# A fused state-space convolution and gated MLP: the second half's 32-row exchange by VectorE copies, spare reload buffers, one pool of PSUM banks, some copies moved between engines, and a new order

## The chip, the cores and the metric

One core of one Trainium2 chip. The metric is the device time in microseconds of one execution; runs are given with their median. The engines are named as the profile names them: PE is TensorE, DVE VectorE, ACT ScalarE, POOL GpSimd, SP the sync engine, which here only issues DMA transfers.

## What is computed

The reference, cut to what matters (x is 2048 tokens by 512 channels, N is 128 modes, F is 1792):

```python
xn = layernorm(x)                                    # per token
dt = exp(log_dt)[:, None]
A, Bc, Cc = A_re + 1j*A_im, B_re + 1j*B_im, C_re + 1j*C_im
K = einsum("dn,dnl,dn->dl", Cc, exp((dt*A)[:, :, None] * l), dt*Bc).real   # l = 0..2047
y = causal_convolution(xn, K) + xn * Dskip           # per channel, by FFT of length 4096
h = sigmoid(xn @ w_gate) * (xn @ w_up)
return x + y + h @ w_down
```

## The kernel before

**Two computations share the core.** The gated MLP is four groups of 512 tokens. A group has 14 gate products (line 1012) and 14 up products (line 1027), each of four 128x512 matmuls into one PSUM bank; ScalarE turns a gate bank into a sigmoid in SBUF (line 1021), and VectorE multiplies it with the up bank (line 1042). For the units that the list `UEV` names, ScalarE first copies the up bank into the tile `us_sb` (line 1038), and VectorE reads that copy instead of PSUM. Four down products of 14 matmuls each (line 1065) end a group; outside the last group ScalarE copies them out (line 1098) and POOL issues an accumulating load that adds x (line 1104).

**The convolution** is done by two short transforms with multiplications between them. First the layernorm is applied in place to the tile `xn` (part of one big SBUF tile). Sixteen first transforms (line 677) leave their results in PSUM pairs (two banks); ScalarE copies a pair out (line 683) and SP stores it to `z_scr` in DRAM. Meanwhile a ladder of twelve squarings (lines 652 to 660, casts to bf16 at line 646) and many complex multiplications on VectorE (lines 717 to 723, seeds copied at line 758) build tables of powers in four blocks of channels (`c` 0 to 3). For each block TensorE contracts the tables (line 806), ScalarE copies the result out (line 812), TensorE rearranges it (line 828), ScalarE copies it into `kT` (line 835) and VectorE adds one row (line 841).

Then come sixteen units: eight of the first 256 channels (`p` 0; blocks 0 and 1) and eight of the second half (`p` 1; blocks 2 and 3). One unit:

1. SP loads a piece of `z_scr` into a buffer zx, TensorE transforms it (line 881), ScalarE copies the pair into half of a buffer xx (line 886).
2. The exchange: four DMA transfers of 64 KB on SP copy each block of 32 partitions of that half to the neighbouring block of 32 partitions in the other half.
3. SP loads a constant E; TensorE multiplies it with `kT` (line 899), ScalarE copies the pair to kb (line 901).
4. VectorE multiplies xx by kb (lines 905 and 909), TensorE transforms back (line 922), ScalarE copies the pair to vs (line 926), and SP stores it to `v_scr`.

At the end both halves of v are reloaded (16 transfers of 256 KB), last transforms (lines 980 and 982) add them to the down products, VectorE adds x (lines 995 and 1085), and SP stores the output.

**What sets the order.** Every step is one operation of a plan (`pl.add`): engine, function, dependencies, slots that it takes and gives back. The cost, the priority and the DMA figures that it is given are not used when the kernel is built. The order is written out by hand as the list `ORDER` of 970 operation numbers; each engine gets its operations in that order and works them off one after the other. The plan hands out slots in that order too, first freed first taken: pairs of PSUM (`s`, two), single banks for gate and up products (`gu`, three), one bank for down products and the warming matmuls (`po`), two zx, three xx, two kb. An operation waits where its slot is still in use. Line 404 issues nearly all transfers, so that tiles tell the transfers apart; the eight transfers in flight on SP's queue each have a semaphore of their own, and a ninth waits for the first.

```python
sws = [dma("SP", lambda xx=xx, b=b: xx()[32 * b:32 * b + 32, 1, :, :],
           lambda xx=xx, b=b: xx()[32 * (b ^ 1):32 * (b ^ 1) + 32, 0, :, :], deps=[ex], prio=QP, pkt=2048, hv=0.5)(64 * KB)
       for b in range(4)]
pa_ = pl.add("DVE", 1.14, fpa, [ek] + sws, PKD, acq=[psl])
```

Of the kernel before, what the change touches and what calls it, by code (L numbers as in the profile page):

```python
# [11 lines left out]
F32 = mybir.dt.float32  # L12
# [20 lines left out]
NH = 41  # L33
# [5 lines left out]
NS, NGU, NPO = 2, 3, 1  # L39
# [136 lines left out]
def _consts():  # L176
# [22 lines left out]
UEV = (17, 21, 24, 25, 28, 29, 30, 31, 32, 33, 34, 35, 36, 37, 38, 39, 40, 41, 42, 44, 45, 46, 47, 49, 51)  # L199
ON_ACT = (0, 2)  # L200
ORDER = [
    2, 42, 21, 18, 44, 43, 0, 3, 1, 23, 22, 47, 45, 9, 10, 17, 5, 32, 24, 14, 33, 25, 46, 48, 26, 4, 6, 34, 27, 35, 29,
    28, 36, 37, 38, 39, 19, 30, 31, 40, 41, 619, 620, 631, 632, 621, 90, 87, 88, 49, 89, 50, 53, 662, 633, 663, 55, 92,
    51, 672, 54, 673, 91, 12, 56, 667, 642, 58, 7, 11, 101, 102, 93, 103, 682, 683, 8, 643, 57, 652, 653, 668, 625,
    657, 626, 669, 670, 59, 658, 622, 623, 627, 15, 61, 671, 60, 63, 97, 664, 113, 624, 677, 678, 659, 639, 640, 62,
    660, 665, 94, 95, 666, 100, 661, 64, 52, 637, 104, 638, 105, 687, 688, 679, 96, 66, 680, 98, 641, 681, 647, 628,
    629, 648, 65, 114, 630, 106, 141, 634, 684, 674, 144, 67, 635, 685, 142, 686, 636, 649, 68, 650, 675, 676, 115,
    644, 689, 131, 651, 654, 70, 167, 143, 145, 214, 109, 69, 108, 655, 132, 645, 690, 646, 215, 691, 134, 71, 72, 107,
    168, 656, 169, 216, 73, 99, 768, 725, 692, 217, 170, 171, 146, 135, 773, 769, 74, 76, 75, 693, 116, 770, 694, 110,
    111, 133, 172, 77, 79, 218, 219, 78, 149, 726, 774, 150, 80, 173, 760, 695, 775, 776, 81, 771, 16, 761, 117, 82,  # L210
    83, 147, 700, 174, 118, 119, 772, 701, 85, 718, 151, 728, 702, 175, 123, 84, 177, 185, 148, 122, 152, 186, 777,
    220, 189, 190, 154, 708, 719, 178, 187, 188, 112, 155, 153, 729, 709, 191, 758, 748, 193, 738, 161, 180, 179, 749,
    720, 182, 721, 739, 183, 759, 710, 194, 195, 733, 722, 750, 164, 165, 162, 751, 136, 196, 711, 734, 740, 197, 121,
    139, 712, 752, 763, 198, 201, 181, 741, 742, 764, 163, 753, 754, 176, 140, 723, 735, 755, 756, 137, 736, 724, 199,
    762, 202, 200, 192, 138, 126, 730, 203, 120, 731, 129, 737, 127, 130, 13, 727, 204, 757, 732, 128, 713, 715, 205,
    714, 86, 184, 743, 156, 716, 717, 159, 124, 206, 221, 222, 744, 157, 745, 765, 766, 746, 747, 767, 160, 207, 209,
    208, 224, 794, 824, 232, 261, 226, 703, 262, 233, 236, 230, 234, 235, 231, 237, 225, 210, 240, 227, 263, 264, 241,
    242, 243, 265, 778, 779, 796, 797, 229, 125, 158, 389, 359, 238, 244, 780, 781, 245, 854, 248, 239, 246, 249, 247,
    360, 390, 391, 361, 786, 434, 782, 223, 855, 787, 211, 250, 435, 228, 436, 440, 212, 266, 251, 252, 253, 788, 795,
    267, 213, 254, 256, 255, 268, 798, 814, 257, 258, 825, 271, 364, 365, 308, 269, 279, 309, 280, 362, 366, 259, 815,  # L220
    393, 260, 394, 274, 275, 281, 826, 804, 441, 358, 363, 396, 395, 439, 827, 273, 367, 442, 829, 859, 438, 310, 283,
    282, 284, 311, 285, 437, 368, 287, 272, 426, 830, 860, 805, 369, 312, 370, 288, 828, 289, 449, 443, 789, 444, 290,
    834, 811, 836, 837, 397, 835, 799, 392, 398, 809, 800, 812, 450, 451, 810, 371, 445, 399, 277, 839, 291, 840, 276,
    292, 813, 838, 831, 819, 372, 832, 295, 820, 293, 801, 802, 419, 381, 833, 294, 286, 400, 427, 821, 822, 428, 880,
    844, 278, 297, 313, 454, 296, 298, 314, 823, 420, 421, 166, 704, 401, 881, 402, 453, 841, 456, 457, 856, 455, 374,
    373, 299, 458, 790, 696, 270, 375, 857, 376, 803, 300, 446, 842, 447, 816, 301, 303, 845, 858, 302, 817, 452, 318,
    315, 459, 818, 326, 317, 323, 460, 424, 422, 425, 411, 378, 379, 380, 327, 843, 330, 304, 319, 885, 806, 807, 846,
    328, 329, 331, 847, 471, 423, 808, 429, 920, 382, 851, 320, 403, 334, 886, 849, 383, 404, 335, 430, 461, 321, 336,
    405, 852, 325, 850, 848, 406, 462, 892, 861, 893, 472, 448, 486, 377, 473, 887, 337, 853, 479, 546, 410, 316, 384,
    431, 338, 432, 862, 480, 20, 339, 385, 340, 863, 341, 305, 481, 342, 888, 322, 344, 324, 306, 882, 412, 332, 433,  # L230
# [17 lines left out]
class _Slot:  # L248
    __slots__ = ("pool", "idx")

    def __init__(self, pool):
        self.pool = pool
        self.idx = None

class _Plan:
# [6 lines left out]
    def add(self, eng, cost, fn, deps=(), prio=0.0, acq=(), rel=(), dma=None, mode="F", tab=None, alt=None):  # L262
# [5 lines left out]
        op.seq = len(self.ops)  # L268
        for d in deps:
            if d is not None:  # L270
                d.users.append(op)
                op.left += 1
        self.ops.append(op)
        return op

    def run(self):

        for n in ORDER or range(len(self.ops)):
            op = self.ops[n]
            for s in op.acq:  # L280
# [875 lines left out]
```

## Time and profile before

| | us |
|---|---|
| median of 3 runs (lowest, highest) | 237.1 (236.8, 238.4) |
| the profiled execution | 238.7 |
| its span | 236.9 |
| ACT busy | 183.8 |
| POOL busy | 22.4 |
| 64 exchange transfers of 64 KB, median from issue to landing | 3.0 |
| 16 z reloads of 256 KB, median | 4.3 |
| 16 v stores of 256 KB, median | 3.6 |
| 12 v reloads on SP's queue, median | 5.5 |

An engine's busy time is the union of its instructions' durations; the mean of one instruction, which the groups give in ns, is longer than its share of the busy time where an instruction starts before the one ahead of it has ended. An idle stretch is put down to the event that came last before it. In the chain of waits each line is one step, with its start, its length, and the engine or transfer that it ran on.

### The profile page before, as it was taken

To read this page: it belongs to the slowest core of one execution; us is meant where nothing else is said; L and a number is where in the kernel's file an instruction comes from. 1 tells how busy PE (TensorE), PEld (TensorE's weight loads), DVE (VectorE), ACT (ScalarE), POOL (GpSimd) and SP (SyncE) were. 2 spreads that over 40 slices of the span, in tenths; PEclk is the share of its full clock that TensorE was granted. 3 is DMA by queue.
4 is the path that set the end of the run, shared out by engine and by line. 5 is a ranking of instruction groups with operands and counts; after the bars stand their busy time and mean duration, and the time that the engine had idled before them with its cause. 6 is when DMAs were issued, how large, how long until landed. Compare 5 with 4: busy or idle time off the path is not lost.

```text
span 236.9 us, 5425 instructions
## 1 busy us (share of the span) xinstructions
PE 217.8 (92%) x2093; PEld 111.0 (47%) x2120; DVE 186.3 (79%) x397; ACT 183.8 (78%) x299; POOL 22.4 (9%) x42
## 2 busy tenths in 40 slices
PE   7977999799999999996999999999899979999693
PEld 2443434244444364454655565556544536444252
DVE  2999999999999999997999999994530561681374
ACT  5999999999999996756999999977557859870000
POOL 1212030040000000670030000000010001000000
PEclk9999999999999999999999999999999999999999
DMA  6999614433624375429887348455698499796965
GB/s 186 330 381 371 201 51 141 121 110 111 133 89 136 129 209 153 82 52 296 209 167 198 79 125 237 117 165 136 174 236 233 119 288 239 206 239 189 297 226 177
DMA packets 47739, 43.46 MB, mean 183 GB/s; under 512 B 9569, under 2 KB 40674, under 8 KB 47714
## 3 DMA queue, kind: packets, MB, share of 16 engines
q1 hardware_dynamic: 45618, 40.43, 57.6%
q0 software_dynamic: 864, 1.57, 4.4%
q10 hardware_dynamic: 1232, 1.11, 1.6%
q8 instruction: 16, 0.26, 0.5%
q14 instruction: 9, 0.07, 0.1%
HBM read 25.28 MB, written 12.06 MB: 158 GB/s over the span
## 4 chain that ended last, share of the span: by engine, by line
PE 46%; ACT 18%; DMA 15%; DVE 14%; issue 4%; SPq 2%; DVEq 0%; ACTq 0%
PE bank L1027 11%; PE bank L1012 11%; PE bank L1065 8%; PE pair L899 7%; DMA big<-z_scr 5%; DVE hT_sb L1042 4%; ACT hT_sb L1021 4%; PE pair L922 3%; PE pair L806 3%; DMA big<-in_A_u_dram 2%; DMA big<-v_scr 2%; SPq L404 2%; ACT big L683 2%; DMA v_scr<-big 2%; PE pair L881 2%
## 5 line engine op out<-in xcount | busy, mean ns | idle before, releaser
L1012 PE MATMUL bank<-xnT,wg_sb 128*128 128x512 bf16 (+1 forms) x223 | 53.6, 368 | 5.9 <-DMA xnT<-x_scr 1.8
L1027 PE MATMUL bank<-xnT,wu_sb 128*128 128x512 bf16 x214 | 53.4, 379 | 1.1 <-ACT hT_sb L1021 0.4
L1065 PE MATMUL bank<-wd_sb,hT_sb 128*128 128x512 bf16 (+1 forms) x234 | 50.9, 367 | 0.2
L1012 PEld LDWEIGHTS <-wg_sb 128*128 128x128 bf16 x236 | 22.0, 97 | 29.9 <-issue 5.7
L1065 PEld LDWEIGHTS <-hT_sb 128*128 128x128 bf16 x238 | 22.6, 98 | 25.7 <-issue 2.4
L1021 ACT ACTIVATE hT_sb<-bank 128x512 bf16<-128x512 f32 x56 | 32.9, 608 | 1.5 <-PE bank L1012 1.5
L905 DVE TENSOR_TENSOR big<-big 128x2048 bf16<-128x2048 bf16 x16 | 19.6, 1224 | 16.9 <-PE pair L922 10.1
L1027 PEld LDWEIGHTS <-wu_sb 128*128 128x128 bf16 x224 | 20.8, 98 | 25.5 <-issue 3.7
L717 DVE TENSOR_TENSOR big<-big 128x1024 bf16<-128x1024 bf16 (+4 forms) x40 | 25.9, 648 | 0.9 <-ACT big L758 0.5
L1042 DVE TENSOR_TENSOR hT_sb<-hT_sb,bank 128x512 bf16<-128x512 bf16 x31 | 20.6, 680 | 6.9 <-PE bank L1027 6.7
L718 DVE TENSOR_TENSOR big<-big 128x1024 bf16<-128x1024 bf16 (+4 forms) x40 | 25.9, 647 | 0.0
L886 ACT ACTIVATE big<-pair 128x1024 bf16<-128x1024 f32 x16 | 16.3, 1024 | 5.4 <-PE pair L881 5.4
L899 PE MATMUL pair<-big 128*128 128x256 bf16 x160 | 19.7, 273 | 0.0
L901 ACT ACTIVATE big<-pair 128x1024 bf16<-128x1024 f32 x16 | 16.3, 1022 | 2.9 <-PE pair L899 2.6
L899 PEld LDWEIGHTS <-big 128*128 128x128 bf16 x160 | 15.5, 98 | 4.7 <-issue 0.2
L926 ACT ACTIVATE big<-pair 128x1024 bf16<-128x1024 f32 x16 | 16.3, 1029 | 1.1 <-PE pair L881 0.5
L722 DVE TENSOR_TENSOR big<-big 128x512 bf16<-128x512 bf16 (+4 forms) x40 | 16.9, 423 | 0.2
L723 DVE TENSOR_TENSOR big<-big 128x512 bf16<-128x512 bf16 (+4 forms) x40 | 16.9, 422 | 0.0
L1038 ACT ACTIVATE us_sb<-bank 128x512 bf16<-128x512 f32 x25 | 14.9, 600 | 2.5 <-PE bank L1027 2.3
L683 ACT ACTIVATE big<-pair 128x1024 bf16<-128x1024 f32 x16 | 16.1, 1047 | 0.4 <-DMA z_scr<-big 0.4
L774 ACT ACTIVATE sq_sb<-big 128x256 bf16<-128x256 bf16 (+2 forms) x20 | 12.9, 646 | 3.9 <-DVE big L723 2.9
L646 ACT ACTIVATE big<-big 128x512 bf16<-128x512 f32 x24 | 13.8, 640 | 0.0
(106 smaller groups left out, 270.4 us busy)
## 6 DMA issues: line engine op xcount, KB each, us to landing
big<-c_E SPq DMA_DIRECT2D x16, 320.0 KB, 3.5
z_scr<-big SPq DMA_DIRECT2D x16, 256.0 KB, 2.6
big<-z_scr SPq DMA_DIRECT2D x16, 256.0 KB, 4.3
big<-big SPq DMA_DIRECT2D x64, 64.0 KB, 3.0
v_scr<-big SPq DMA_DIRECT2D x16, 256.0 KB, 3.6
big<-v_scr SPq DMA_DIRECT2D x12, 256.0 KB, 5.5
big<-in_A_u_dram SPq DMA_DIRECT2D x4, 512.0 KB, 8.0
wu_sb<-in_B_w_up_dram SPq DMA_DIRECT2D x2, 896.0 KB, 10.6
```

The costliest lines, as they stand in the source:

```text
L683: ev = pl.add("ACT", 0.90, lambda sl=sl, zs=zs: S.activation(out=zs().rearrange("p j d -> p (j d)"), in_=two(sl), func=ACT.Identity), [fx_ ...
L717: V.tensor_tensor(out=wide(outp), in0=wide(lo), in1=mre, op=ALU.mult)
L718: V.tensor_tensor(out=wide(tb()), in0=wide(lo), in1=mim, op=ALU.mult)
L722: V.tensor_tensor(out=outp[:, :, :, 0, :], in0=outp[:, :, :, 0, :], in1=tb()[:, :, :, 1, :], op=opr)
L723: V.tensor_tensor(out=outp[:, :, :, 1, :], in0=outp[:, :, :, 1, :], in1=tb()[:, :, :, 0, :], op=opi)
L899: T.matmul(two(sk)[:, o:o + DW], es()[:, g, kt, :], kT[p][:, kt, :], start=kt in (0, NKT - 1), stop=kt >= NKT - 2)
L905: V.tensor_tensor(out=pp().rearrange("p q h m -> p (q h) m"), in0=xx().rearrange("p q h m -> p (q h) m"), in1=kb()[:, 0:2 * DW].unsqueeze( ...
L1012: T.matmul(bank(sl)[:, c0:c1], w[:, kt, k * 128:(k + 1) * 128], xnT[:, grp, kt, c0:c1], start=(kt == 0), stop=(kt == KT - 1))
L1021: S.activation(out=hT_sb[:, hs.idx, k % 2, :], in_=bank(sl), func=ACT.Sigmoid)
L1027: T.matmul(bank(sl), wu_sb[:, kt, k * 128:(k + 1) * 128], xnT[:, grp, kt, :], start=(kt == 0), stop=(kt == KT - 1))
L1042: V.tensor_tensor(out=h(), in0=h(), in1=us_sb[:, us.idx, :] if on else bank(sl), op=ALU.mult)
L1065: T.matmul(bank(po)[:, 0:c[1] - c[0]], hT_sb[:, hts[k // 2].idx, k % 2, jj * 128:(jj + 1) * 128], wd_sb[:, k, c[0]:c[1]], start=first and ...
```

## The change

- The exchange of the second half's units (`p` 1) is four VectorE copies instead of four transfers; the first half's stays on SP.
- When the last table contraction has run, memory that the tables used is handed to the pools: a fourth buffer xx and eight more zx. A unit takes its xx when it copies into it, no longer when z is loaded. The reloaded v are laid out by half first, so that the extra zx lie where the second half's v go.
- The bank `po` joins the pool `gu` (four banks) for gate, up and down products and the warming matmuls.
- Copies that ScalarE made go through `pl.copy`, which puts an operation on VectorE if its number is in `ON_DVE`: four casts of the ladder, seven of twelve layernorm applications, nine small table copies and three pair evictions of the second half (two into xx, one into vs). `UEV` has 37 units instead of 25.
- The last down products no longer name the last transform back as a dependency.
- `ORDER` is new (946 operations). Of what moves: SP loads x first and the first parameters fourth; the load of w_down stands behind the first x and z stores and the first transposing load; the third set of five warming matmuls stands before the first gate; three down products of the third group stand before the last table contraction instead of behind it.

```diff
-NS, NGU, NPO = 2, 3, 1
+NS, NGU = 2, 4
-UEV = (17, 21, 24, 25, 28, 29, 30, 31, 32, 33, 34, 35, 36, 37, 38, 39, 40, 41, 42, 44, 45, 46, 47, 49, 51)
+UEV = (0, 2, 4, 5, 9, 10, 14, 15, 16, 18, 19, 20, 23, 24, 25, 27, 28, 29, 30, 31, 32, 33, 34, 36, 37, 38, 39, 40, 41, 42, 43, 44, 47, 50, 51, 52, 54)
+ON_DVE = (54, 57, 60, 84, 96, 107, 108, 110, 120, 121, 123, 167, 177, 179, 180, 182, 214, 230, 273, 308, 481, 565, 573)
...
+    def copy(self, nc, cost, out, in_, *args, **kw):
+
+        get = lambda v: v() if callable(v) else v
+        dve = len(self.ops) in ON_DVE
+
+        def fcopy():
+            if dve:
+                nc.vector.tensor_copy(out=get(out), in_=get(in_))
+            else:
+                nc.scalar.activation(out=get(out), in_=get(in_), func=ACT.Identity)
+        return self.add("DVE" if dve else "ACT", cost, fcopy, *args, **kw)
...
-            if i >= LN_ACT:
+            dve = i < LN_ACT or len(pl.ops) in ON_DVE
+            if not dve:
...
+            if dve:
+                V.tensor_copy(out=W[p][:, k], in_=cur[:, :, DW * p:DW * p + DW])
...
+    kgen[3][0].rel += tuple(_Slot(k, i) for k, n, m in (("xx", 3, 4), ("zx", 2, 10)) for i in range(n, m))
...
             lx = dma("SP", zx, z_v[:, u, :, dsl], deps=fx_st + xn_free, prio=QP,
-                     acq=[xsl, zsl], pkt=512, hv=0.49)(256 * KB)
+                     acq=[zsl], pkt=512, hv=0.49)(256 * KB)
...
+            ex = pl.copy(nc, 0.91, lambda xx=xx: xx()[:, 0].rearrange("p h (g d) -> p g h d", g=2),
+                         lambda sl=sl: two(sl).rearrange("p (g h d) -> p g h d", g=2, h=2), [mm], QP, acq=[xsl], rel=[sl])
+            half_of = lambda xx, b, q: xx()[32 * b:32 * b + 32, q, :, :]
+            if p == 0:
+                sws = [dma("SP", lambda xx=xx, b=b: half_of(xx, b, 1), lambda xx=xx, b=b: half_of(xx, b ^ 1, 0), deps=[ex], prio=QP,
+                           pkt=2048, hv=0.5)(64 * KB) for b in range(4)]
+            else:
+                def f_sw(xx=xx):
+                    for b in range(4):
+                        V.tensor_copy(out=half_of(xx, b, 1), in_=half_of(xx, b ^ 1, 0))
+                sws = [pl.add("DVE", 1.5, f_sw, [ex], QP)]
...
-    vall = at(0, [8, NP, 2, 2, DW])
-    vps = [[vall[:, t, p] for t in range(8)] for p in range(NP)]
+    vall = at(0, [NP, 8, 2, 2, DW])
+    vps = [[vall[:, p, t] for t in range(8)] for p in range(NP)]
...
-            pos = [_Slot("gu" if late and jj % 2 else "po")] + [_Slot("gu")] * last
+            pos = [_Slot("gu") for _ in range(1 + last)]
...
-                            prods + [l_wd] + ([md] if jj else []) + ([mv_] if late else []) + pre_, DP, acq=[] if last else [po],
+                            prods + [l_wd] + ([md] if jj else []) + pre_, DP, acq=[] if last else [po],
```

## The prediction

> **What bounds the kernel now.** I read the page's totals and slices first, then busy time by stage, then the chain of waits, then the groups by shape.
>
> ```profile
> PE 217.8 (92%) x2093; PEld 111.0 (47%) x2120; DVE 186.3 (79%) x397; ACT 183.8 (78%) x299; POOL 22.4 (9%) x42
> ...
> PE   7977999799999999996999999999899979999693
> ...
> DVE  2999999999999999997999999994530561681374
> ACT  5999999999999996756999999977557859870000
> ```
>
> TensorE is the bound: its 217.8 us of matmul stay whatever the change does, so only its 19.1 us of idle time can be won, 3.6 of it after the last matmul. VectorE is full until about 165 us and then half empty; ScalarE is full until 88.
>
> ```profile
> core 0: us, PE busy (x) PEld busy (x) DVE busy (x) ACT busy (x) POOL busy (x), PEclk, DMA share, GB/s
> 0.00:13.68 13.68, 11.20 (x54) 5.14 (x55) 8.50 (x30) 10.57 (x19) 2.46 (x12) 1.00 0.86 278
> 13.68:44.10 30.42, 26.21 (x138) 12.06 (x140) 29.82 (x63) 30.33 (x51) 4.40 (x6) 1.00 0.66 213
> ...
> 136.34:160.14 23.80, 23.39 (x343) 13.36 (x346) 23.67 (x52) 21.53 (x37) 0.89 (x3) 1.00 0.57 159
> 160.14:211.50 51.36, 48.41 (x581) 26.86 (x588) 23.87 (x39) 36.51 (x49) 1.73 (x2) 1.00 0.78 207
> 211.50:236.90 25.40, 19.73 (x120) 9.56 (x121) 11.37 (x15) 1.93 (x3) 0.00 (x0) 1.00 0.71 224
> ```
>
> Stages, cut at the first gate matmul (13.68), the end of group 0 (44.10), the last table matmuls (160.14) and the last unit's product (211.50). Up to 160.14 TensorE idles 10.5 us, in the second half 3.0, in the tail 5.7. The granted clock is 1.00 in all of them.
>
> ```profile
> 162.10 4.38 DMA big<-z_scr
> ...
> 190.77 1.24 DVE big L905
> ...
> 212.87 4.46 DMA v_scr<-big
> ...
> 217.96 5.22 DMA big<-v_scr
> ```
>
> The chain of waits names what TensorE waited for late: a reload of z (two buffers only; 1.02 us lost at 166.5), a product behind the exchange (1.35 us lost at 192), and at the end the last v store and its reload.
>
> **The start.** SP issues its loads in another order: the first parameter load moves from first to fourth, behind x tiles 0 to 7. It took 3.1 us. With it 1,408 KB are queued; the present fifth load has 1,440 KB queued and took 6.5 us (issued 2.6, landed 9.1). So I put it at 8.7 us instead of 3.9. ScalarE's queue still has exp and sin ahead of the two evictions into xnT: exp 0.63, two VectorE multiplies 1.3, exp 0.61, table load 1.28, four sin steps 2.47: 6.3 us, so the evictions start at 15.0 instead of 12.72. Cost 2.3 us; bounds 0 (3.1 us as now) and 5 (9.9 us, the second parameter load). Five warming matmuls (1.2 us, formerly at 151) fill part of it. The load of w_down moves behind the first x and z stores and the first transposing load. By the durations of ScalarE's queue SP reaches it at 33 us. As it took 15.9 us among the other loads, and its 1,792 KB are 5 us at the 330 to 381 GB/s that the page gives for 6 to 24 us, it lands between 40 and 49; the first down group comes at about 44. I take 41 and no cost, since no other large load is left by then; the late end would cost 5.
>
> **Before the last table.** ScalarE loses 4 casts (2 x 0.575), 7 normalisations (0.825), 9 small table copies (0.43) and 3 pair evictions (1.02), and gains 12 us copies (0.60): -4.6 -5.8 -3.9 -3.1 +7.2 = -10.2 us. The rest of that comes in the first 88 us, where it is full: ahead of the first table's eviction its queue is 4 us shorter.
>
> VectorE, up to the end of the last table, gains the casts (nearest row 128x512 f32 at 0.42, so 4 x 0.84; up to 0.69 if they go as two-operand f32), the normalisations (the same instruction as L543, 0.37 busy), the small copies (nearest two-operand row 0.29; I take 0.24), and 11 products fewer from PSUM (0.665) with 12 more from us (0.416): 3.4 + 2.6 + 2.2 - 7.3 + 5.0 = +5.9 us (between +4 and +8). The last table ended on VectorE at 159.7, so it ends at 165.6, or 164 if the 1.45 us wait of L841 at 111.9 goes. TensorE has three down groups more (3.02 each) and one gate and one up fewer (0.86) queued ahead of it: +7.3. So VectorE's delay is covered if TensorE idles no more than 7 to 8 us there.
>
> TensorE's idle time up to there was 10.5: 2.5 before 13.68, 4.2 to 44.10, 3.8 later. The start makes 3.6 of the 2.5. The 1.76 us wait for xnT goes: its store came at 33.7, 19 us after the evictions into xnT, and now has some 9 us of ScalarE work behind them ahead of it; one z store fewer stands before its transposing load on SP. Of 2.4 us of waits for a free bank I take half, since gate and up products now rotate over four banks, and down groups share them, so a bank held 3.0 us by a down group can also cost as much. Of the 1.47 us before the second selection, two thirds. Sum 10.5 + 1.1 - 1.8 - 1.2 - 1.0 = 7.6. TensorE reaches the last table at 149.7 (its busy time so far) + 7.3 + 7.6 = 164.6, VectorE at 164 to 165.6: I take 164.8.
>
> **Second half.** It loses the three down groups and gains an up: 48.4 - 9.1 + 0.9 = 40.2 us of TensorE. Eight z loads may run ahead (five slots are used past the first two, all freed by the last table matmuls), so the z wait goes; 32 SP issues of 0.5 us and their 3.0 us landings go. In their place VectorE makes 32 copies of 32x1024.
>
> ```profile
> L905 DVE TENSOR_TENSOR big<-big 128x2048 bf16<-128x2048 bf16 x16 | 19.6, 1224 | 16.9 <-PE pair L922 10.1 <-ACT big L901 3.0 <-DMA big<-big 2.9
> ...
> L718 DVE TENSOR_TENSOR big<-big 128x1024 bf16<-128x1024 bf16 x16 | 11.0, 688 | 0.0
> ...
> L543 DVE TENSOR_SCALAR big<-big,ln_m_f,ln_ri_f 128x512 bf16<-128x512 bf16 x4 | 1.5, 409 | 0.0
> ...
> L604 DVE TENSOR_SCALAR big<-big 128x512 f32<-128x512 f32 x1 | 0.4, 419 | 0.0
> ```
>
> No row is a wide bf16 copy. Two operands of this length take 0.69, one operand of half of it 0.41 (0.33 start to start). So four copies cost 1.3 to 2.75 us; one element a cycle, as L995 from PSUM with 1.22 for 1024, would make 4.9. I take 2.0, between the two SBUF rows, since a copy has no second stream and no scalar to read. Until the last unit VectorE then has 10 x 1.225 + 10 x 0.68 for products, 8 x 2.0, three evictions at 1.2, six products 3.0 and a small row 0.3: 42 us, where it had 23.9 in a longer stage. TensorE's 40.2 and about 2.5 of waits make 42.7. Among these: the first pair eviction on VectorE waits for unit 8, whose z load SP issues only behind a v store, about when the table matmuls start (4.4 us of load, 2.7 of cover). Behind it in VectorE's queue stands the row addition that all K products of this half wait for: up to 2 us. They are level; each 0.1 us more per exchange past 2.1 adds 0.8 us. Last unit at 207.5 (was 211.5).
>
> [...]
>
> **Tail.** Behind the last product TensorE has one gate and two ups where it had two ups, so 0.9 us more of the v store and reload is hidden (0.93 was idle at 220.7), and 0.9 us more work is left: nothing either way. The 25.4 us stay. The new layout of the v buffers lets z lie where the second half's v come last; it adds no instruction. On POOL the prefix sums (some 6 us) move behind the last memset at about 165 and are needed some 25 us later: nothing.
>
> Span 207.5 + 25.4 = 232.9. The profiled execution took 238.7 (span 236.9 and 1.8 around it), so it would be 234.7, 4.0 less. The median of the runs is 237.1, 1.6 below the profiled one: 237.1 - 4.0 = 233.1.
>
> **Rivals.** *VectorE becomes the bound* of the second half: slower. It speaks for it that it has 42 us against 42.7, in a fixed order, where a late exchange also holds the products, and two evictions that free a PSUM pair. It decides from 2.1 us per exchange; at 2.75 the time is 238.3, from 2.9 it is over 1% slower, at 3.3 it is 242.7, at 4.9 some 255. Against it: VectorE's half idle stage, and rows that all lie below 0.7. *The new order does not fit the chip*: the late parameters cost 2.3 us (up to 5) and the shared banks win nothing, so TensorE idles as before up to the last table; VectorE's +5.9 then sets it at 165.6 to 167.5, and the time is 235 to 240, 237 likeliest. For it: ScalarE and VectorE have no slack in the first 88 us. *The exchange was hidden anyway*: then only the earlier work counts; z's 1.0 and the product's 1.35 stay lost, 235.4.
>
> **How the numbers follow.** 1% (2.4 us) is what can be told from no change. The forecast, 229 to 234.7, gets 0.55. The order that does not fit 0.22: 0.05 faster, 0.12 within, 0.05 slower. VectorE as the bound 0.16: 0.03 within, 0.13 slower. The hidden exchange 0.07: 0.03 faster, 0.04 within. Sums: faster 0.63, same 0.19, slower 0.18. About 0.07 lies below 229 and 0.12 above 240, so the range is 229 to 240.
>
> **What would show it.** First gate matmul near 16.0 us, not 13.7; no wait for xnT near 44; the last table's matmuls at 164 to 166 with some 7.6 us of TensorE idle before; copies of 32x1024 at 0.45 to 0.55 us; VectorE over 90% full from there to the last unit's product at 207 to 208; about 25 us behind it. I am wrong if the copies take over 0.55 us or the last table comes after 168.

## The result and the profile after

The changed kernel takes 236.06 us (median of 20 runs, 234.39 to 238.51) beside 237.36 us for the kernel before (also 20 runs): ratio 0.994, 95% interval 0.991 to 0.997. The prediction was 233.1. The forecast gain of 4 us became 1.3, a third of it.

The profiled execution took 238.2 us with a span of 236.4. The page of the changed kernel, its totals and slices:

```profile
PE 220.5 (93%) x2092; PEld 112.3 (47%) x2120; DVE 205.9 (87%) x456; ACT 175.4 (74%) x284; POOL 19.4 (8%) x42
...
PE   7959999999899999999999999999699999997794
...
DVE  3799999999979999999999998998679989960474
...
PEclk9999999999999999999999999999889999999799
```

VectorE is now full into the second half, as meant. New are two dents in the row of the granted clock, near 170 and 222 us; the kernel before had none. Busy time by stage, cut as before (first gate matmul, end of group 0, last table matmuls, end of the last unit's product):

```profile
core 0: us, PE busy (x) PEld busy (x) DVE busy (x) ACT busy (x) POOL busy (x), PEclk, DMA share, GB/s
0.00:16.41 16.41, 12.60 (x58) 5.59 (x60) 10.86 (x35) 10.68 (x19) 2.46 (x12) 1.00 0.89 300
...
163.22:207.85 44.63, 41.59 (x544) 23.64 (x549) 39.06 (x70) 32.29 (x43) 4.17 (x9) 0.96 0.76 206
207.85:236.40 28.55, 22.22 (x127) 10.88 (x125) 12.71 (x17) 2.59 (x4) 0.00 (x0) 0.94 0.52 166
```

| stage, us | predicted | changed kernel | kernel `both` (below) |
|---|---|---|---|
| to the first gate matmul | 16.0 | 16.41 | 15.35 |
| to the last table matmuls | 148.8 | 146.81 | 147.67 |
| second half | 42.7 | 44.63 | 42.02 |
| behind the last product | 25.4 | 28.55 | 24.16 |
| span | 232.9 | 236.40 | 229.20 |

Up to the last table the kernel is 1.6 us ahead of the prediction. It loses 1.9 in the second half and 3.15 in the tail. TensorE's waits, largest first (total, how often, longest), name both places:

```profile
PE pair L991 <- DMA big<-v_scr: 2.9, 1, 2.9
...
PE pair L838 <- issue: 1.3, 1, 1.3
```

In the timeline the first loss lies inside the last selection (the matmuls that rearrange a table result, line 828 before and 838 now), which stops after 50 of 64 matmuls with everything it reads in place; the second ahead of the first last transform:

```profile
166.75 0.74 PE L838 MATMUL pair<-big,sw 128*32 128x96 bf16 x50 [0.51 <-ACT big L285]
168.80 0.35 PE L838 MATMUL pair<-big,sw 128*32 128x96 bf16 x14 [1.31 <-issue]
...
220.02 0.62 PE L991 MATMUL pair<-big 128*64 128x512 bf16 x4 [2.94 <-DMA big<-v_scr]
```

Busy time by stretch behind each of the two; the third column from the end is the granted clock, 0.50 for some 3 us:

```profile
169.80:173.00 3.20, 2.98 (x9) 1.22 (x9) 2.90 (x6) 0.80 (x2) 0.00 (x0) 0.50 0.50 79
```

```profile
221.00:224.00 3.00, 3.00 (x16) 1.57 (x13) 2.19 (x3) 0.00 (x0) 0.00 (x0) 0.50 0.37 110
```

At the clock of 0.50 six gate matmuls (line 1023, from 170.10 us) took 2.77 us, where eight at 1.00 took 1.89 to 1.90 (180.69 and 193.10): half the pace. TensorE then does in 3.2 us what takes 1.6, so by my estimate each fall costs up to 1.6 us. Not every execution has both falls: the two runs whose mean clock was 1.00 had spans of 232.4 and 232.8 us, the six at 0.983 to 0.986, the profiled one among them, had 234.0 to 236.4, so the table shows the losses of a long execution.

### The profile page after: what moved, and what is told of

Same layout as the page of the kernel before. It is cut to its first block, busy times and chain, and to the rows that moved or that the text cites. A ratio compares the mean times of both kernels' runs of the same rounds, so it can differ in the third digit from the quotient of the medians.

```text
span 236.4 us, 5411 instructions
## 1 busy us (share of the span) xinstructions
PE 220.5 (93%) x2092; PEld 112.3 (47%) x2120; DVE 205.9 (87%) x456; ACT 175.4 (74%) x284; POOL 19.4 (8%) x42
## 4 chain that ended last, share of the span: by engine, by line
PE 51%; DVE 14%; ACT 14%; DMA 13%; issue 4%; SPq 2%; ACTq 0%; DVEq 0%
PE bank L1076 13%; PE bank L1038 9%; PE bank L1023 9%; PE pair L912 6%; DMA v_scr<-big 5%; PE pair L818 5%; ACT big L285 4%; PE pair L934 4%; ACT big L662 3%; DMA big<-in_A_par_dram 3%; ACT big L668 2%; DVE big L609 2%; DMA big<-v_scr 2%; SPq L416 2%; DMA z_scr<-big 2%
## 5 line engine op out<-in xcount | busy, mean ns | idle before, releaser
L285 ACT ACTIVATE big<-pair 128x1024 bf16<-128x1024 f32 (+2 forms) x73 | 70.7, 986 | 18.4 <-PE pair L818 5.5
L1076 PE MATMUL bank<-wd_sb,hT_sb 128*128 128x512 bf16 (+1 forms) x232 | 50.3, 367 | 0.3
L733 DVE TENSOR_TENSOR big<-big 128x1024 bf16<-128x1024 bf16 (+4 forms) x40 | 25.7, 642 | 0.8 <-ACT big L285 0.5
L1049 ACT ACTIVATE us_sb<-bank 128x512 bf16<-128x512 f32 x37 | 22.6, 614 | 0.8 <-PE bank L1038 0.5
L1053 DVE TENSOR_TENSOR hT_sb<-hT_sb,us_sb 128x512 bf16<-128x512 bf16 x37 | 15.2, 415 | 0.5 <-ACT us_sb L1049 0.5
L903 DVE COPY big<-big 32x1024 bf16<-32x1024 bf16 x32 | 13.4, 419 | 0.6
L1006 DVE TENSOR_TENSOR big<-pair,glu_sb 128x1024 bf16<-128x1024 f32 x4 | 4.8, 1221 | 10.2 <-PE pair L991 10.2
L1053 DVE TENSOR_TENSOR hT_sb<-hT_sb,bank 128x512 bf16<-128x512 bf16 x19 | 12.9, 681 | 0.6 <-PE bank L1038 0.3
L934 PE MATMUL pair<-big 64*64 64x512 bf16 (+1 forms) x256 | 13.1, 327 | 0.1
```

The source lines that it names most:

```text
L285: nc.scalar.activation(out=get(out), in_=get(in_), func=ACT.Identity)
L733: V.tensor_tensor(out=wide(outp), in0=wide(lo), in1=mre, op=ALU.mult)
L934: T.matmul(two(sv)[o:o + 64, DW * (2 * g + y):2 * DW * (g + 1)], mab[b:b + 64, 2 * u + g, q, :], pq()[b:b + 64, q, ch] if y else pp()[b:b ...
L1049: S.activation(out=us_sb[:, us.idx, :], in_=bank(sl), func=ACT.Identity)
L1053: V.tensor_tensor(out=h(), in0=h(), in1=us_sb[:, us.idx, :] if on else bank(sl), op=ALU.mult)
L1076: T.matmul(bank(po)[:, 0:c[1] - c[0]], hT_sb[:, hts[k // 2].idx, k % 2, jj * 128:(jj + 1) * 128], wd_sb[:, k, c[0]:c[1]], start=first and ...
```

## The experiments

**The tail.** The first suspicion fell on the new layout. The last transform of a block of tokens reads both halves of v with one access. In the old layout that is 4 KB in one piece; in the new one it is a range of 16 KB and more, which takes in other blocks. In the program as compiled, the first last transform waits for seven transfers' semaphores in the changed kernel and for three in the old layout. `v_by_token`:

```diff
-zx=[OFF["zs"], OFF["zs"] + 2 * KB] + [16 * KB + 2 * KB * i for i in range(8)])
+zx=[OFF["zs"], OFF["zs"] + 2 * KB] + [2 * KB + 4 * KB * i for i in range(8)])
-    vall = at(0, [NP, 8, 2, 2, DW])
-    vps = [[vall[:, p, t] for t in range(8)] for p in range(NP)]
+    vall = at(0, [8, NP, 2, 2, DW])
+    vps = [[vall[:, t, p] for t in range(8)] for p in range(NP)]
-            T.matmul(o[64 * j:64 * j + 64, :], s2[:, r, :], vall[:, ps, t, j, r, :], ...
+            T.matmul(o[64 * j:64 * j + 64, :], s2[:, r, :], vall[:, t, ps, j, r, :], ...
```

> The changed kernel with one thing undone: the v buffers lie token block by token block again (both halves of a block side by side), and the extra z places take the second half's 2 KB of each block instead of one 16 KB region. No instruction is added or taken away. Theory (a wait by address range): in the changed kernel the last transform of block 2 reads one range that reaches over the places of blocks 3 to 7 of the first half and 0 to 2 of the second, so it waits for the reload of block 1, the last one issued, and lands at 220.02; with the old layout it waits for its own two loads (the second half's block 2 was issued at 213.01 and took 4.8 us), so it starts near 218, idle before it falls from 2.94 to about 1 us, the granted clock behind it stays at 1.00 where it was 0.50 for 3.2 us, and the stretch from the last unit's product to the end is about 25 us instead of 28.55. Time 232.3 to 233.5, 2.5 to 3.7 less than the changed kernel's 236.06, ratio to before near 0.981. Rival A (the reload is late by itself, since eight loads share the DMA engines): the first last transform still starts at 219.5 or later and the time stays at 235.5 to 236.5. Rival B (the clock falls for another reason than this wait): the start moves to 218 but the clock still falls to 0.5 behind it; 234 to 234.8.

Measured: 233.39 us, ratio 0.987 (0.982 to 0.991). The timeline of `v_by_token` in the tail:

```profile
208.92 6.22 PE L1076 MATMUL bank<-wd_sb,hT_sb 128*128 128x512 bf16 x28
215.58 0.62 PE L991 MATMUL pair<-big 128*64 128x512 bf16 x4 [0.45 <-DMA big<-v_scr]
217.03 0.59 PE L991 MATMUL bank<-big 128*64 128x512 bf16 x3 [0.83 <-DMA big<-v_scr]
```

The one wait of 2.94 us has become small ones (a third, of 0.52, follows), each for the block that is needed next, and the clock stays at 1.00. The median is inside the expected span, the ratio a little above it. The wait by address range is the cause; rivals A and B are out. Its size varies, though. The four profiles with the new layout wait 2.94, 2.67 (`par_first`), 2.9 (`warm_tail`, most of it filled) and 1.24 us ahead of the first last transform; the nine with the old layout wait 0.45 us there (`v_by_token`) or not at all. The short one is `fetch_shift`:

```profile
215.83 0.62 PE L991 MATMUL pair<-big 128*64 128x512 bf16 x4 [1.24 <-DMA big<-v_scr]
```

There the clock stays at 1.00 as well, and from the last product to the end it takes 25.7 us, as long as `v_by_token`. The nine with the old layout take 24.0 to 25.7 us, so the new one cost less than 2 us in that execution and 2.9 us or more in the profiled one, the fall of the clock included.

**The clock by itself.** `warm_tail` leaves the layout and the wait, and fills most of the wait with matmuls:

```diff
+    def f_wt():
+        for _ in range(10):
+            T.matmul(bank(wtl), glu_sb[:, 0, 0:128], glu_sb[:, 0, :], start=True, stop=True)
+    pl.add("PE", 1.5, f_wt, (), 0, acq=[wtl], rel=[wtl])
```

> The changed kernel with ten more matmuls of 128x512 on constant weights, whose result nobody reads, put into TensorE's wait ahead of the first last transform (2.1 us of work). The wait for the reload stays. Theory (an idle stretch of nearly 3 us makes the granted clock fall): the first last transform starts near 220.0 as before, but the clock stays at 1.00 behind it, so the end comes 1.4 to 1.7 us sooner: 234.2 to 234.8. Rival A (the clock falls for another reason, the load on the chip or the narrow matmuls): it falls to 0.5 as before and the time is 236 or a little over. Rival B (the end is bound by the output stores, so TensorE's slow stretch costs nothing): clock 1.00 and still 236.

Measured: 235.65 us, ratio 0.994 (0.991 to 0.997). The timeline of `warm_tail` at the filled wait, and its busy time by stretch behind it:

```profile
214.93 2.32 PE L1121 MATMUL bank<-glu_sb 128*128 128x512 bf16 x10
217.96 0.62 PE L991 MATMUL pair<-big 128*64 128x512 bf16 x4 [0.71 <-DMA big<-v_scr]
```

```profile
217.90:221.00 3.10, 2.96 (x23) 1.58 (x23) 2.38 (x4) 0.00 (x0) 0.00 (x0) 1.00 0.03 4
221.00:224.00 3.00, 2.92 (x14) 1.13 (x12) 1.19 (x3) 0.00 (x0) 0.00 (x0) 1.00 0.94 302
```

With 0.71 us of the idle stretch left, the clock stays at 1.00, and none of the twelve runs has a mean clock under 0.991, where six of the twenty of the changed kernel have 0.983 to 0.986. So the idle stretch can make the clock fall. It need not: in `par_first` the clock stays at 1.00 behind 2.67 us at the same place.

```profile
220.85 0.62 PE L991 MATMUL pair<-big 128*64 128x512 bf16 x4 [2.67 <-DMA big<-v_scr]
```

The time hardly moves, which misses the expected 1.4 to 1.7 us. In this execution TensorE, at full clock, waited 0.89 us for a later reload instead, and the clock fell at 167 to 172 us as in the changed kernel. How much of the tail's fall the reload would have cost anyway is not settled.

**The stop in the selection.** The kernel before had such a stop too, 1.47 us inside its second selection:

```profile
108.51 0.65 PE L828 MATMUL pair<-big,sw 128*32 128x96 bf16 x43
110.63 0.42 PE L828 MATMUL pair<-big,sw 128*32 128x96 bf16 x21 [1.47 <-issue]
```

Counted in TensorE's compiled order (matmuls and weight loads), the two come ahead of instructions 1723 and 3259, and both numbers leave 187 when divided by 256. `fetch_shift` moves all numbers by 168 without adding columns:

```diff
-                T.matmul(bank(wsl), glu_sb[:, 0, 0:128], glu_sb[:, 0, :], start=True, stop=True)
+                T.matmul(bank(wsl)[:, 0:w], glu_sb[:, 0, 0:128], glu_sb[:, 0, 0:w], start=True, stop=True)
-    warm = [keep_warm(28, -10)]
+    warm = [keep_warm(112, -10, 128)]
```

> The changed kernel with its 28 first warming matmuls of 128x512 cut into 112 of 128x128: the same columns, 168 more instructions (matmuls and weight loads) ahead of everything else on TensorE. Theory (the 1.31 us stop inside the last selection, and the 1.47 us one inside the second selection of the kernel before, are TensorE's sequencer waiting for its next block of instructions: both stops come at an instruction number that leaves 187 when divided by 256, 1723 and 3259, in a stretch where nearly 400 short instructions follow one another while loads fill the DMA engines): with the numbers moved by 168 the boundary falls into the table matmuls, the block after it is needed only behind the selection, and no stop of over 0.5 us is left in the selections; the granted clock stays at 1.00 from 163 to 175 where the profile showed 0.50 for 3.2 us. The profiled execution's second half (last table to last unit's product) is 42 to 43 us instead of 44.6; the median of the runs moves by 0 to -0.8, since most runs of the changed kernel have only one fall of the clock, the one in the tail. Rival A (the stop belongs to the instruction, an operand or a semaphore): it stays behind the 50th matmul of the last selection. Rival B (it belongs to the load on the DMA engines alone): a stop of 1 us or more comes anywhere in 166 to 169 us.

Measured: 234.47 us, ratio 0.987 (0.983 to 0.991). The second and the last selection in the timeline of `fetch_shift`:

```profile
111.30 0.82 PE L838 MATMUL pair<-big,sw 128*32 128x96 bf16 x59
112.56 0.24 PE L838 MATMUL pair<-big,sw 128*32 128x96 bf16 x5 [0.44 <-issue]
...
166.80 0.87 PE L838 MATMUL pair<-big,sw 128*32 128x96 bf16 x64 [0.30 <-ACT big L285]
```

So the last selection runs through. A short stop has come in the second one, ahead of instruction 1981, which leaves 189. With the instructions that only wait for a semaphore counted too, all three places leave the same remainder, 194: the new place is that of a boundary to the instruction. All three profiles that keep the changed kernel's numbers up to there (`v_by_token`, `warm_tail`, `par_first`) stop behind the same 50th matmul, for 1.88, 1.06 and 2.06 us, so it is in every profile seen, and the gain (0.7% by the ratios, 1.6 us by the medians) is larger than the 0.8 us expected at most. Rival A is out. So is B as it stands, for the stop keeps to an instruction number; that it needs loaded DMA engines as well is left open.

`both` has the two edits together.

> The changed kernel with the old v layout (z places moved into the second half's places of it) and the 28 warming matmuls cut into 112, that is the edits of v_by_token and fetch_shift together. Theory (the false wait for v and the stop at an instruction block are two separate losses that the prediction did not have): no stop over 0.5 us in the last selection, the waits ahead of the first last transforms together below 2 us, the granted clock at 1.00 in all stages; second half 42 to 42.7 us, 25.2 to 26.7 behind it; time 231.5 to 232.8, ratio to before 0.976 to 0.980. Rival (one loss hides the other: when the second half ends sooner, the reload still needs its 10 us behind the last v store, and VectorE, 93% full, takes back the stop): 233.2 to 234, as with either edit alone.

Measured: 230.82 us, ratio 0.973 (0.968 to 0.979): a shorter time than with either edit alone, and shorter than expected. Its second half and tail, busy time by stage:

```profile
163.02:205.04 42.02, 40.59 (x544) 23.52 (x550) 39.52 (x72) 32.24 (x43) 4.82 (x9) 1.00 0.79 221
205.04:229.20 24.16, 20.53 (x125) 9.91 (x125) 12.55 (x17) 2.59 (x4) 0.00 (x0) 1.00 0.59 194
```

The clock is 1.00 throughout, and the two losses do not hide one another: by the ratios the gain over the changed kernel is 2.1%, where each edit alone brings 0.7%. What goes beyond their sum is not clear of the intervals. A stop is left in the second selection, at the place where `fetch_shift` has one:

```profile
112.31 0.24 PE L838 MATMUL pair<-big,sw 128*32 128x96 bf16 x5 [0.90 <-issue]
```

This kernel is faster than the kernel before and the changed one.

**Can the boundary be put where it does no harm?** `best` moves the numbers by 136 (96 warming matmuls of 128x149).

> The kernel of both with the 28 first warming matmuls cut into 96 of 128x149 instead of 112 of 128x128, so that the instruction numbers move by 136 instead of 168. In the profiles so far each stop ends 4.2 to 5.3 us after TensorE passed the instruction number one block (256) earlier; so a stop comes wherever TensorE runs through 256 instructions in less time than that. Theory: by the durations of the matmuls, 168 leaves one such place (118 instructions into the second selection, where both stopped 0.90 us) and 136 leaves none. No stop of over 0.25 us in any selection or table; 0.4 to 1 us less than both's 230.82, ratio to before 0.968 to 0.973. Rival (blocks do not set it; another place takes the stop): one stop of 0.5 us or more elsewhere, and no less time than both.

Measured: 231.11 us, ratio 0.975 (0.970 to 0.980), no better than `both`. In its timeline TensorE stops inside the last table (the profiled execution took 234.1 us, 3.0 more than the median, so the stop need not be as long in all):

```profile
162.11 2.63 PE L818 MATMUL pair<-big 128*32 128x82 bf16 x114 [0.57 <-DVE big L738]
167.03 0.47 PE L818 MATMUL pair<-big 128*32 128x82 bf16 x14 [2.29 <-issue]
```

114 matmuls into the table is instruction 3259 once more, so the place is right and the rule for the length was wrong. The boundary before it was passed at 158.3 us, 8.7 us ahead of the restart and not 4.2 to 5.3. The block itself (one packet of 16 KB on an instruction queue) moved at 164.5 to 165.0 us, while the DMA engines had been idle from 157 to 160: the request went out later than I had it. In this kernel that boundary lies 28 instructions ahead of the table, which waited for VectorE until 162.11; what lets the request go out is not shown.

**Does the stop cost the kernel before anything?** `before_shift` is the kernel before with 122 warming matmuls of 128x117.

> The kernel before the change, with nothing altered but its 28 warming matmuls, cut into 122 of 128x117: the instruction numbers move by 188. Theory (the stop of 1.47 us in its second selection has the same cause): that stop is gone; a shorter one may come in the last table's place, where two boundaries are some 3.5 us apart, if the DMA engines are loaded there. Time 235.9 to 236.8, ratio to before 0.993 to 0.998. Rival (in this kernel the stop is covered, since VectorE's ladder sets the last table): no change, ratio 0.998 to 1.002, with the 1.47 us turned into another wait before the last table.

Measured: 238.42 us, ratio 1.008 (1.005 to 1.011). The second selection runs through, and the next K product (E times `kT`) comes 3 us behind it in the timeline of `before_shift`:

```profile
108.97 0.87 PE L828 MATMUL pair<-big,sw 128*32 128x96 bf16 x64
...
113.08 2.12 PE L899 MATMUL pair<-big 128*128 128x256 bf16 x16 [1.41 <-DMA big<-c_E]
```

The stop was covered there: that product waits for its E load, which did not come sooner. The rival is right in kind. Why this kernel is even slower is open; its first gate came 0.5 us later.

**The start.** `par_first` moves one number, the first parameter load, back to the head of `ORDER`.

> The changed kernel with the first parameter load put back to the head of SP's queue, everything else as it is. Theory (the prediction's: the late parameters cost 2.3 us which nothing takes back, as TensorE is full behind the start): par0 lands near 4 us, the first gate matmul comes at 13.7 to 14.2 instead of 16.4, and the last table matmuls at 161 to 162 instead of 163.2; time 233.7 to 234.5. Rival A (x tiles 0 to 3 come 0.6 us later and their statistics then set the first gate): 15 or later, gain under 1 us. Rival B (ScalarE and VectorE set the pace up to 88 us, so an earlier first gate only moves idle time to later waits for xnT and the table casts): first gate at 14, last table still at 163, time 235.5 to 236.3.

Measured: 237.10 us, ratio 0.996 (0.993 to 1.000). The load landed at 3.94 us and the first gate matmul came at 16.87, later than without. The multiplications that need the exponential of the parameters, and what is ahead of them in the timeline of VectorE in `par_first`:

```profile
9.29 0.68 DVE L543 BATCH_NORM_STATS2 stats<-big 128x6 f32<-128x512 bf16 x1
10.01 0.18 DVE L544 BATCH_NORM_AGGREGATE mv<-stats 128x2 f32<-128x6 f32 x1
10.11 1.27 DVE L609 TENSOR_TENSOR big<-big 128x512 f32<-128x512 bf16 x2
```

They stand behind three tiles' statistics in VectorE's queue, and the x tiles now landed later. So the early load did nothing, TensorE was idle 2.50 us ahead of the transposes, and its clock was 0.50 from 15 to 18 us. That is rival A, and worse than it had. (One profile each: in the ten other profiles with the changed kernel's order of loads the first gate comes between 15.2 and 16.3 us, so half a microsecond is within what executions differ by.) `start_old` moves the first 30 or so operations with the load, on the kernel of `both`:

```diff
 ORDER = [
-    0, 23, 22, 19, 1, 33, 24, 25, 32, 34, 9, 2, 3, 35, 26, 89, 36, 42, 43, 45, 44, 37, 39, ...
+    2, 42, 44, 43, 0, 3, 1, 23, 22, 47, 45, 9, 19, 32, 24, 33, 25, 46, 48, 26, 34, 27, 35, ...
```

> The kernel of both with the start of the kernel before: the first parameter load at the head of SP's queue and the first 30 or so operations in the old order on every queue, so that the two parameter multiplications stand ahead of the first x statistics on VectorE and exp ahead of the squares on ScalarE (par_first moved the load alone, and the multiplications then waited in VectorE's queue). Theory (the prediction's first term: the late start is a pure loss of 2.3 us, since TensorE is full behind it): first gate matmul at 13.6 to 14.2 us where both has 15.35 and the changed kernel 16.41, and the last table's matmuls sooner by as much; time 1.2 to 2 us less than both's 230.82, ratio to before 0.965 to 0.970. Rival (ScalarE and VectorE, each over 98% full from 16 to 44 us, set the pace there, so TensorE starts sooner and waits more): first gate near 14, waits for sigmoids and us copies of 1 us or more before 44 us, time within 0.6 us of both.

Measured: 231.10 us, ratio 0.973 (0.969 to 0.978), as `both`. The first gate came at 14.75 us instead of 15.35, and TensorE's timeline in `start_old` shows 0.80 lost to a piece of w_gate, which stands later in SP's queue than in the kernel before:

```profile
17.49 4.06 PE L1023 MATMUL bank<-xnT,wg_sb 128*128 128x512 bf16 x20 [0.80 <-DMA wg_sb<-in_B_w_gate_dram]
```

The last table began at 162.96 against 163.02. Neither side is quite met: the start came only 0.6 us sooner, which is little beside that spread, and it was lost to a load and not to ScalarE. What 2 us at the start would bring stays open.

**The exchange.** `swap_twice` makes each copy of `both` twice.

```diff
-                    for b in range(4):
+                    for b in (0, 1, 2, 3, 0, 1, 2, 3):
                         V.tensor_copy(out=half_of(xx, b, 1), in_=half_of(xx, b ^ 1, 0))
```

> The kernel of both with each of the 32 exchange copies on VectorE made twice (64 copies of 32x1024 at 0.419 us; the result is the same). It adds 13.4 us to VectorE in the second half, where the profiles have VectorE busy for 38.6 of 41.3 us and TensorE for 40.3. Theory (as the prediction has it, the two engines are level there, so what is put on VectorE comes out as time): the second half ends 10 to 12.5 us later, time 242 to 245. Rival (VectorE's queue runs ahead of TensorE and the exchange has slack): 3 us or less. The size between tells how much slack the exchange had: each us of slack per half lowers the growth by 1 us.

Measured: 244.97 us, ratio 1.033 (1.028 to 1.038), which is 14.2 us more than `both` for 13.4 us more copies. Busy time in the second half of `swap_twice`:

```profile
163.04:218.60 55.56, 44.43 (x543) 24.55 (x549) 51.86 (x95) 32.22 (x43) 4.48 (x9) 0.94 0.61 171
```

VectorE is busy for 51.9 of 55.6 us. The exchange has no slack: a microsecond of copies is a microsecond of time, and a little more, since TensorE then waits up to 2.96 us at once and the clock falls (0.94 over these 55.6 us, 1.00 in `both`).

`swap_dma` puts the exchange of `both` back on SP's queue, with the four issues directly behind the eviction that they read:

```diff
-                        V.tensor_copy(out=half_of(xx, b, 1), in_=half_of(xx, b ^ 1, 0))
-                sws = [pl.add("DVE", 1.5, f_sw, [ex], QP)]
+                            Y.dma_start(out=half_of(xx, b, 1), in_=half_of(xx, b ^ 1, 0))
+                sws = [pl.add("SP", 1.5, f_sw, [ex], QP)]
```

> The kernel of both with the second half's exchange made by four 64 KB DMAs on SP's queue, as the kernel before has it, issued directly behind the eviction they read; all else in the same order. VectorE loses 13.4 us of the second half. Theory (the prediction's: the exchange on DMA costs some 3 us of latency per unit, which the order can hide for most units as it lies 2 to 13 VectorE operations ahead of the product, and TensorE with 40.3 us is then the bound): the second half stays at 41.5 to 44 us and the time at 230 to 233; the VectorE copies by themselves then bring little. Rival (SP's queue, in which z loads, E loads, stores and reloads stand behind the exchange's wait for its eviction, becomes the bound, at 32 issues of 0.5 us more): 4 to 10 us more than both, with TensorE waiting for z, E or the exchange.

Measured: 256.59 us, ratio 1.081 (1.074 to 1.088), far beyond the rival's 4 to 10 us. The waits of SP's queue and of TensorE in the second half of `swap_dma`:

```profile
SPq L904 <- ACT big L285: 13.8, 2, 9.0
```

```profile
PE pair L890 <- DMA big<-z_scr: 5.8, 2, 4.4
PE pair L913 <- DMA big<-c_E: 5.1, 1, 5.1
```

SP stood up to 9.0 us at a time before an eviction that it was to send on, with z and E loads behind it in its queue. In this order the exchange cannot go back. The kernel before carries it on SP, so the loss belongs to the pair of order and queue, not to the transfers.

**The extra z places.** `two_z` is `both` with two places, and unit 11's load moved behind the transform of unit 12.

> The kernel of both without the eight extra z places: two, as in the kernel before, with the one load that would then find no place (unit 11) moved behind the transform of unit 12 in the order. Theory (in the new order at most three z tiles are under way at a time, so the eight places are used one after the other and not at once): 0 to 0.5 us more than both, TensorE's waits for z below 0.5 us. Rival (the prediction's reading, that loads running ahead take the wait for z away): a wait for z of 1 us or more per unit comes back in the second half, 1 to 4 us more.

Measured: 232.67 us, ratio 0.984 (0.980 to 0.988): 1.9 us more than `both` by the medians, 2.5 by the ratios. One wait for z came back in the timeline of `two_z`:

```profile
185.07 0.41 PE L890 MATMUL pair<-big,m 64*64 64x512 bf16 x4 [1.51 <-DMA big<-z_scr]
```

The order never has more than three z tiles under way, but the third place is worth one wait. Neither reading was right: it comes once, not per unit. (In this profile TensorE also waits 1.06 us for a reload in the tail, where `both` waits 0.36; no run tells whether the z places have to do with that.)

**The copies moved to VectorE.** `copies_on_act` is `both` with `ON_DVE = ()`.

> The kernel of both with the 23 copies and normalisations that the change put on VectorE (4 casts, 7 normalisations, 9 small table copies, 3 pair evictions) back on ScalarE, in the same order of operations. Theory (ScalarE, full in 16 to 44 us and the engine that fed the first table before, gets 12 to 13 us more, some 9 of them before 90 us; VectorE, which is full there too, gets 11 to 12 us less): the first table comes later than the 86 us of the changed kernel by 2 to 5 us and the time grows by 2 to 5 us. Rival A (only the sum over the two engines counts up to 88 us and both are full, so it is moved in vain): within 0.7 us. Rival B (VectorE was the tighter one, with 116 of 119 us up to the last table): 1 us or more faster.

Measured: 242.62 us, ratio 1.023 (1.018 to 1.028): 11.8 us more, against 2 to 5 expected. Busy time in two stages of `copies_on_act`:

```profile
16.60:44.00 27.40, 24.52 (x129) 11.30 (x131) 20.64 (x43) 26.96 (x47) 4.20 (x6) 1.00 0.66 209
44.00:90.00 46.00, 39.71 (x205) 16.88 (x208) 35.44 (x83) 45.60 (x80) 3.51 (x6) 1.00 0.34 99
```

ScalarE is full up to 90 us, VectorE empties, and the first table comes at 95.4 instead of 85.0. In this order nearly all the ScalarE time that the change took away is on the path. No run takes the single pool of banks, the longer `UEV` or the dropped dependency away by itself, so what each of these is worth stays open.

**The order of the tail.** `both_d14` puts the down groups of tiles 14 and 15 further ahead among the last transforms.

> The kernel of both, with TensorE's order in the tail changed: the down group of token tile 14 goes directly behind the first last transform instead of behind the fourth, and the down group of the first half of tile 15 behind the fourth instead of behind the sixth. Theory (the waits left in the tail, 0.4 to 1.2 us ahead of the first last transform and 1.1 us behind it, are for the reloads, and 3.1 us of down work covers those behind the first): 0.7 to 1.2 us less than both. Rival A (VectorE's additions of 1.22 us behind each last transform then come in a row and hold TensorE, which has two pairs for them): no change within 0.4 us. Rival B (the stores of the output come later and the end waits for them): 0.5 to 1 us more.

Measured: 231.67 us, ratio 0.977 (0.972 to 0.981), no faster than `both`. TensorE no longer waits for reloads, but 0.37 and 0.52 us for VectorE's additions (line 1006): rival A.

## Why the prediction was off

**The step that failed** is the one on the tail: the layout "adds no instruction", so "nothing either way. The 25.4 us stay." An edit that adds no instruction can still change which bytes an access spans, and with them what it waits for. The stretch took 28.55 us in the profiled execution, 3.15 more than forecast, with a wait of 2.94 us and a fall of the clock in it; `v_by_token` with the old layout alone took off 2.7 us by the medians, 1.7 by the ratios to the kernel before.

**The second term missed** is in "TensorE's 40.2 and about 2.5 of waits make 42.7". The TensorE work was right (40.6 in `both`) and so was the sum, where nothing stops: 42.02. The changed kernel took 44.63, since its instruction numbers put a boundary of 256 inside the last selection. The change did not make this kind of stop, it moved it from a place where an E load covers it (`before_shift`) to one where nothing does. I had seen the 1.47 us of before as "issue" and counted two thirds of it as gained.

Neither sign of being wrong that the prediction names came: the copies took 0.42 us and the last table stood at 163.22. Both misses lie outside what these signs watch. Without them its sum was even too high: `both` takes 230.82 us where the forecast is 233.1. Its last table comes at 163.02 against 164.8, its second half is 0.7 us and its tail 1.2 us shorter than forecast.

**Right by the runs:**

- The exchange copy took 0.419 us, in this row of the changed kernel's groups (busy us, mean ns):

```profile
L903 DVE COPY big<-big 32x1024 bf16<-32x1024 bf16 x32 | 13.4, 419 | 0.6
```

- So it was 1.68 us per exchange and not the 2.0 that I took from the nearest rows. The busy time is 32 times the mean, so no copy overlaps the next.
- VectorE as the level partner of TensorE: 39.5 of 42.0 us in `both`, and `swap_twice` shows the slope behind the level.
- No wait for xnT near 44 us; w_down's late load cost nothing.
- The last table, which came at 163.22 against 164.8 with no wait ahead of it: VectorE's delay was covered as forecast, and TensorE had idled 6.5 us up to there, not 7.6.

**Right in number, not in reason:** the first gate (16.0 against 16.41, and 15.35 in `both`). The parameter load landed at 8.94 us as forecast (8.7), but `par_first` shows that an early load moves nothing while VectorE's queue keeps its order. The extra z places took the wait away as said, though with one place and not with eight.

**Of the rivals,** "the order does not fit the chip" gave the right time (235 to 240) by a wrong mechanism: TensorE's waits for a bank up to the last table fell from 1.7 to 1.1 us, and that table came early. The exchange was not hidden: in the order of `both` its copies come out as time (`swap_twice`).

## What to carry over

A new layout can change what an access waits for even where it adds no instruction (here a wait of 2.94 us in place of 0.45): look at the range between the first and the last byte that an access touches, and at whose buffers lie inside it. A stretch of short matmuls should be looked at with its instruction numbers, for a boundary of 256 instructions in it stopped TensorE for 0.9 to 2.3 us in eight profiles here. Cutting warming matmuls shifts the boundary; it helped where the stop had been on the path (1.6 us by the medians in `fetch_shift`), but in `best` the stop only moved to another place, and in `before_shift` it was covered. Moving a load ahead was worth nothing here while the work that needs it stood behind other work on its engine, and two losses nearly as large as the gain can leave a good change looking like no change.

## What the runs showed of the hardware

- **TensorE can stop at a boundary of 256 instructions.** Eight profiles of the changed kernel and its variants stopped 0.9 to 2.3 us at one; four others stopped 0.2 to 0.6 us at the same place of the second selection as `both`. The DMA queue of kind "instruction" (q8) moved 16 packets of 16 KB in the changed kernel, which has 4,212 matmuls and weight loads in its profile, and 17 in `fetch_shift`, with 168 instructions more: about one packet for every 256. In the changed kernel one of them moved between 166.50 and 167.50 us, and TensorE went on behind its stop at 168.80. In the eight, TensorE came from one boundary to the next in 3.1 us (the changed kernel) to 6.4 us (`best`).
- **The clock can fall after less than 3 us of idle time.** It was 0.50 for about 3.4 us (in the changed kernel, both times) behind 2.94 us of idle time, and fell likewise behind 2.50 (`par_first`), behind 2.96 (`swap_twice`), behind 2.29 and 0.47 close together (`best`), behind 0.51 and 1.31 (the changed kernel) and behind 0.51 and 1.06 (`warm_tail`); but it stayed at 1.00 behind 2.67 (`par_first`, in the tail), behind 2.25 (`swap_twice`), behind 0.51 and 1.88 (`v_by_token`) and behind 1.76 alone (the kernel before). So these runs give no threshold.
